# A transformer block's first segment: half of its modulation columns by tensor-engine products, and one written order for all engines

## The chip, the cores and the metric

The kernel runs on one core of a Trainium2 chip. The metric is the device time of one execution in microseconds. TensorE (PE in the profile, its weight loads PEld) multiplies, VectorE (DVE) and ScalarE (ACT) work elementwise, GpSimd (POOL) helps, and SyncE (SP) issues the transfers.

## The reference

The block takes 2048 tokens of width 1024. A vector `c` gives six modulation rows by a product with `w_mod`; two of them scale and shift the normalised input ahead of the attention, two ahead of the feed-forward part, and two gate the branches. The attention works in four segments of 512 tokens, each with softmax inside the segment and a memory of the segments before it.

```python
mod = (_silu(c) @ w_mod).reshape(c.shape[0], 6, 1, -1)
sa, ca, ga, sb, cb, gb = (mod[:, 0], mod[:, 1], mod[:, 2], mod[:, 3], mod[:, 4], mod[:, 5])
h = _layernorm(x, axis=-1) * (1 + ca) + sa
x = x + ga * _A_ref(h, A_wq, A_wk, A_wv, A_wo, A_beta)
h = _layernorm(x, axis=-1) * (1 + cb) + sb
x = x + gb * _B_ref(h, B_w_gate, B_w_up, B_w_down)
```

In `_A_ref`, q, k and v are products of h with 1024 x 1024 weights, 32 heads of 32; `_B_ref` is `(gelu(h @ w_gate) * (h @ w_up)) @ w_down` with 3584 hidden units.

## The kernel before

**Numbers.** Products with float32 accuracy are made of three float32r products: each operand is cut into a high half (a copy rounded to float32r, on ACT) and a low half (the difference, on DVE or POOL). `split_w` (L194 to L202) cuts weights, `mm` (L361) issues the three products of one block of 128 rows.

**The attention** goes through 32 steps (`steps`): for each half of the sequence and each of eight groups of four heads, two segments. A step has scores S, values V, memory M and A, and beside it the products K (v, then k) and Q of the next step; two written strings, `ORDER0` for the first step and `ORDER` for the others, interleave these pieces on TensorE. Weights of the next group are fetched and cut as entries of a list `todo` at positions of that string. After the steps come the output projection and the feed-forward part.

**Who sets the order.** TensorE runs in the order of the program throughout (`tc.manual_schedule`). In the first segment SP does so too. DVE, ACT and POOL there, and all but TensorE in the attention steps, are ordered by a planner that goes by its own costs and by what is ready; SP, and then the others, are in program order again in the feed-forward part. A wait between engines is a semaphore; a buffer of a pool (`tag`, `bufs`) is reused when its last reader is done.

**The first segment.** The set-up loads `ccol` (c), `bb` (beta), the eight half tiles of the first 512 tokens (`x0`), and the first group's weights wq, wv, wk into three of the four `raw` buffers. It makes selectors (`ident`, `pick`, `eye`, `sel4`, `selj`, `seli`, `blk`) and the causal `mask`, the silu of c (`scol`), a row copy of it in all partitions (`scb`, by `row_of`), and the gates (`gall`, `omg`).

A modulation column is 128 values of one row of `mod`; `modT[:, r]` holds column r, where columns 0 to 7 are the shift `sa` and 8 to 15 the scale `ca`, one of each for every block `kt` of 128 features. `mod_load` fetches 128 x 1024 values of the transposed `w_mod` (512 KB) into one of eight `spare` buffers; `mod_col` (L187) multiplies them by `scb` and sums along the row in one DVE instruction, and adds 1 to a scale. All sixteen columns of the first two rows are made so, in the order of `kt`:

```python
order = [r for kt in range(KT) for r in (8 + kt, kt)]
for i, r in enumerate(order):
    mod_col(*got[i])
    if i + 8 < len(order):
        got.append(mod_load(order[i + 8], spare[i % 8]))
```

`norm_seg_stats` normalises four tiles of tokens: statistics on DVE (L232 to L237), a power on POOL (L238), the scaling of both halves on ACT (L245). `norm_seg` (L325) turns a block of features by four transposes (L329), modulates it on ACT with columns `kt` and `8 + kt` (L331), and cuts it into high (L334, ACT) and low (L335, DVE). `first_part` multiplies each block with the three weights (L365, 72 products), and ends with `k_out`, `v_out`, `q_out` (copies and cuts of k, v and q), `k_turn` and `v_turn`. The transfers of k into `ks` are issued in `k_turn` (L395), those of q in `q_out` (L421). Meanwhile the second segment's tokens (`x1`, four `raw` buffers) are loaded and normalised; their `norm_seg` runs as the piece N of the first step. After `first_part` come the fills of the last 32 partitions of `ks` (L1361).

Of the kernel before, what the change touches and what calls it, by code (L numbers as in the profile page):

```python
# [11 lines left out]
F32 = mybir.dt.float32  # L12
# [7 lines left out]
P = 128  # L20
D = 1024
# [12 lines left out]


@with_exitstack
def block_kernel(ctx: ExitStack, tc: tile.TileContext, x, c, wmod, wq, wk, wv, wo, beta, wg, wu, wd, out):
    nc = tc.nc
    f32 = lambda ap: ap.bitcast(F32)

# [50 lines left out]

    ccol = cs([P, KT], "ccol")
    nc.sync.dma_start(ccol, c)
    bb = cs([P, H], "bb")
    nc.sync.dma_start(bb, bass.AP(tensor=beta.tensor, offset=beta.offset, ap=[[0, P], [1, H]]))
    def fetch(src, name):
        r = raw_tile("r" + name)
        nc.sync.dma_start(r, src)
        return r

    x0 = [[], []]
    for i in range(4):
        for h in range(2):
            tag, bufs = ("pt0", 4) if h == 0 else ("sj", 3) if i < 3 else ("pq", 2)
            t = t2(f"x0_{i}_{h}", tag, bufs=bufs)
            nc.sync.dma_start(t, x[i * P:(i + 1) * P, h * L:(h + 1) * L])
            x0[h].append(t)
    raw0 = [fetch(w[0], f"w0_{i}") for i, w in enumerate((wq, wv, wk))]


    ones = cs([P, P], "ones")
    nc.vector.memset(ones, 1.0)
    ident = cs([P, P], "ident")
    nc.gpsimd.affine_select(ident, ones, pattern=[[-1, P]], compare_op=ALU.is_equal, fill=0.0,
                            base=0, channel_multiplier=1)
    mask = pa.tile([P, L], F32, name="mask")
    nc.vector.memset(mask, 0.0)
    nc.gpsimd.affine_select(mask[:, L - P:], mask[:, L - P:], pattern=[[-1, P]],
                            compare_op=ALU.is_ge, fill=MASK, base=0, channel_multiplier=1)

    pick = tmp_tile("pick")[:, :P].rearrange("p (j d) -> p j d", d=DH)
    nc.gpsimd.affine_select(pick, ones.rearrange("p (j d) -> p j d", d=DH), pattern=[[-1, 4], [-4, DH]],
                            compare_op=ALU.is_equal, fill=0.0, base=0, channel_multiplier=1)
    sel4 = cs([P, 4], "sel4")
    nc.vector.tensor_reduce(sel4, pick, axis=AX.X, op=ALU.add)
    blk = pa.tile([P, P], F32, name="blk")
    nc.vector.tensor_copy(blk.rearrange("p (j e) -> p j e", e=DH), sel4.unsqueeze(2).to_broadcast([P, 4, DH]))

    eye = tmp_tile("eye")[:, :32].rearrange("p (j i l) -> p j i l", j=4, i=4)
    nc.gpsimd.affine_select(eye, ones[:, :32].rearrange("p (j i l) -> p j i l", j=4, i=4),  # L130
                            pattern=[[-8, 4], [-2, 4], [-1, 2]], compare_op=ALU.is_equal, fill=0.0,
                            base=-96, channel_multiplier=1)
    selj = cs([P, 4], "selj")
    nc.vector.tensor_reduce(selj, eye.rearrange("p j i l -> p j (i l)"), axis=AX.X, op=ALU.add)
    seli = cs([P, 4], "seli")
    nc.vector.tensor_copy(seli, eye[:, 0, :, 0])
    for j in range(4):
        for part in range(2):
            if j or part:
                nc.vector.tensor_add(seli, seli, eye[:, j, :, part])  # L140
    mhalf = cs([P, 4], "mhalf")
    nc.vector.memset(mhalf, -0.5)


    def sigmoid(dst, src):
        nc.scalar.activation(dst, src, AF.Exp, scale=-1.0)
# [18 lines left out]
    def row_of(*a):  # L165
        for _ in row_parts(*a):
            pass

    scol = cs([P, KT], "scol")
    sigmoid(scol, ccol)  # L170
    nc.vector.tensor_mul(scol, scol, ccol)
    scb = t2("scb", "row", shape=(P, D))
    row_of(scb, scol, tmp_tile, "sc")
    gall = cs([P, H], "gall")
    sigmoid(gall, bb)
    omg = pa.tile([P, H], F32, name="omg")
    nc.vector.tensor_scalar(omg, gall, -1.0, 1.0, op0=ALU.mult, op1=ALU.add)
    modT = cs([P, 48], "modT")

    def mod_load(r, w=None):  # L180
        if w is None:
# [133 lines left out]
            for _ in range(3):  # L315
                yield

    def norm_seg_stats(s, halves, tiles=range(4)):

        for i in tiles:  # L320
            mv, rs = norm_stats([halves[0][i], halves[1][i]], f"a{s}_{i}", s > 0)
            norm_scale([halves[h][i] for h in range(2)], mv, rs, f"{s}_{i}")
# [37 lines left out]
    def mm(i, ps, g, s, kt):  # L360
# [3 lines left out]
        for a, b in ((0, hi), (0, lo), (1, hi)):  # L364
            nc.tensor.matmul(ps, w[:, a], b, start=(kt == 0 and a == 0 and b is hi), stop=(kt == KT - 1 and a == 1))  # L365

    def v_out(n, nm, ps):
# [4 lines left out]
        ST[n] = [None, ks_t[n % 2], vx, None]  # L372
        return vr, vx

    def v_turn(nm, vr, vx):
# [5 lines left out]
    def k_out(s, nm, ps):  # L381
# [7 lines left out]
            nc.scalar.activation(kr, ps, AF.Copy)  # L389
        return kh, kl, kr  # L390

    def k_turn(n, s, nm, kh, kl, kr):
        ks = ks_t[n % 2]
        for qd, srct in ((0, kh), (1, kh), (2, kl)):
            nc.sync.dma_start(f32(ks[32 * qd:32 * qd + 32]), f32(srct))  # L395
        if s < NSEG - 1:
            ps = s_ps("kT" + nm)
            for t in range(4):
                nc.tensor.transpose(ps[:, t * P:(t + 1) * P], kr[:, t * P:(t + 1) * P], ident)
            e = tmp_tile("ek" + nm)  # L400
            nc.scalar.activation(e, ps, AF.Exp)
            nc.vector.tensor_scalar_min(e, e, 1.0)
            pk = t2("pk" + nm, "pk", shape=(P, 4, P))
            nc.vector.scalar_tensor_tensor(pk.rearrange("p a b -> p (a b)"), ps, 0.0, e, op0=ALU.max, op1=ALU.add)
            PK[n] = pk, ST[n][2]

    def q_out(n, s, nm, ps):
# [14 lines left out]
        ST[n][0], ST[n][3] = qs, pq  # L422

    def kv_part(n, g, s):

        nm = f"{g}_{s}"
        ps = mm_ps("v" + nm)
        for kt in range(KT):
            mm(1, ps, g, s, kt)
            if kt % 2 and kt < KT - 1:  # L430
                yield
        vr, vx = v_out(n, nm, ps)
        yield
        ps = mm_ps("k" + nm)
# [19 lines left out]
        q_out(n, s, nm, ps)  # L454
        yield

    def first_part(n, g, s):

        nm = f"{g}_{s}"
        pv, pk, pq = mm_ps("v" + nm), mm_ps("k" + nm), o_ps("q" + nm)  # L460
        for kt in range(KT):
            for i, ps in ((1, pv), (2, pk), (0, pq)):
                mm(i, ps, g, s, kt)
            yield
        kk = k_out(s, nm, pk)
# [868 lines left out]
    proj = projections()  # L1334
    gab = None
    with tc.manual_schedule(engines={mybir.EngineType.PE}):
        with tc.manual_schedule(engines={mybir.EngineType.SP}):
            free = [wsp_tile("wm_a"), wsp_tile("wm_b")] + [
                t2(f"wm_{q}", "qs", bufs=2, dt=F32R, shape=(P, 4, L)).rearrange("p (a b) t -> p a (b t)", a=2) for q in "cd"]
            spare = [f32(w[:, h]) for w in free for h in range(2)]  # L1340
            order = [r for kt in range(KT) for r in (8 + kt, kt)]
            got = [mod_load(r, spare[i]) for i, r in enumerate(order[:8])]
            norm_seg_stats(0, x0)
            W[0] = [None] * 3
            for i in (1, 2, 0):
                W[0][i] = split_w(raw0[i], wsp_tile(f"w0_{i}"), nc.vector)
            nseg = norm_seg(0, x0)
            for i, r in enumerate(order):
                mod_col(*got[i])
                if i + 8 < len(order):  # L1350
                    got.append(mod_load(order[i + 8], spare[i % 8]))
                if i in (1, 3):
                    next(nseg)
            x1h = [fetch(x[L + i * P:L + (i + 1) * P, :], f"x1_{i}") for i in range(4)]
            x1h = [[t[:, h * L:(h + 1) * L] for t in x1h] for h in range(2)]
# [4 lines left out]
        for k in ks_t:  # L1360
            nc.scalar.activation(k[96:128], selj[96:128].unsqueeze(2).to_broadcast([32, 4, L]), AF.Copy)  # L1361
        norm_a = norm_tiles(x, hT_d, (2, 3), 1, 0, "a")
        next(norm_a)
        for n in range(len(steps) + 1):
# [7 lines left out]
            work["N"] = norm_seg(1, x1h) if n == 0 else norm_a  # L1372
            side = none
            if n in (14, 15):
                hT[n - 12] = []
# [91 lines left out]
```

## Time and profile before

| what | value |
|---|---|
| median of 3 runs | 2791.91 us (2790.25 to 2795.36) |
| profiled execution | 2793.34 us |
| its span, first to last instruction | 2791.6 us |
| mean granted clock of TensorE | 0.994 |
| busy share | PE 98%, PEld 79%, DVE 63%, ACT 46%, POOL 19% |
| instructions | 38457 |
| moved by DMA | 480.17 MB, mean 172 GB/s |

The span is what the trace shows; the execution has 1.7 us around it. A busy share is an average over the whole span: the first segment is some 2% of it and looks different from the rest. In rows of the timeline the start and the length are in microseconds; "x3" counts the instructions in a row, and brackets hold the idle time ahead and what ended it.

### The profile page before, as it was taken

The page shows a single profiled execution, that of the slowest core. Times are in us where ns is not written, and L with a number is a line of the kernel's source. Part 1 is how long each engine was busy: PE and PEld are TensorE (multiplying, and loading weights), DVE is VectorE, ACT ScalarE, POOL GpSimd, SP SyncE. Part 2 cuts the span into 40 slices and gives each one's busy share as a digit, 9 for nine tenths or more (in the row PEclk, how much of TensorE's full clock was granted, in tenths as well). Part 3 has the DMA queues.
Part 4 walks back from the last instruction along what each step waited for, and adds up shares of the span by engine and source line. Part 5 has one row for each costly group of instructions (what it writes and reads, how often), then busy time and mean ns, then how long its engine had stood idle before and what let it go on. Part 6 is the DMA issues. An engine that isn't in the chain of part 4 may idle for free.

```text
span 2791.6 us, 38457 instructions
## 1 busy us (share of the span) xinstructions
PE 2726.0 (98%) x13276; PEld 2206.7 (79%) x13276; DVE 1762.9 (63%) x3727; ACT 1291.4 (46%) x2861; POOL 542.2 (19%) x986
## 2 busy tenths in 40 slices
PE   5999999999999999999999999999999999999999
PEld 4777777777777777788888887888888878888887
DVE  7566566766666744677776768666678754434543
ACT  6688776767676635233433324223223243232220
POOL 0333334333332531100000002000000002112432
PEclk8999999999999999999999999999999999999999
DMA  7566655666555547655655644343567685544652
GB/s 228 129 147 139 157 114 127 148 141 128 114 115 101 133 169 250 210 205 194 226 197 204 234 161 157 137 149 129 190 246 249 218 312 171 184 139 155 207 185 79
DMA packets 229606, 480.17 MB, mean 172 GB/s; under 512 B 17442, under 2 KB 92194, under 8 KB 229410
## 3 DMA queue, kind: packets, MB, share of 16 engines
q1 hardware_dynamic: 229408, 477.72, 56.9%
q8 instruction: 104, 1.70, 0.3%
q14 instruction: 94, 0.75, 0.1%
HBM read 300.96 MB, written 126.35 MB: 153 GB/s over the span
## 4 chain that ended last, share of the span: by engine, by line
PE 85%; DVE 7%; DMA 3%; ACT 2%; issue 2%; POOL 1%; SPq 0%; DVEq 0%; ACTq 0%; POOLq 0%
PE f L1126 36%; PE d L1292 19%; PE k L365 6%; PE q L365 5%; PE v L365 4%; PE y L630 3%; PE S L498 3%; PE O L571 3%; PE T L562 3%; DVE qs L515 1%; PE M L478 1%; PE R L585 1%; DVE sj L500 1%; DVE A L764 1%; PE num L536 1%
## 5 line engine op out<-in xcount | busy, mean ns | idle before, releaser
L1126 PE MATMUL f<-A,B 128*128 128x512 f32 x4704 | 1074.6, 390 | 4.9 <-DVE c L1091 3.2
L1126 PEld LDWEIGHTS f<-A,B 128*128 128x128 f32 x4704 | 882.6, 188 | 190.3 <-issue 2.9
L1292 PE MATMUL d<-wb,ah 128*128 128x512 f32 x2352 | 534.4, 389 | 1.0 <-DVE wb L1177 1.0
L1292 PEld LDWEIGHTS d<-wb,ah 128*128 128x128 f32 x2352 | 441.3, 188 | 93.8 <-DVE wb L1177 1.8
L500 DVE CUSTOM_DVE_ANT_0 sj<-S,mask 128x384 f32<-128x384 f32 (+3 forms) x512 | 227.9, 487 | 183.8 <-PE S L498 175.3
L502 ACT ACTIVATE sj<-sj,mm 128x384 f32<-128x384 f32 (+3 forms) x512 | 282.4, 556 | 27.5 <-DVE mm L500 25.2
L564 ACT ACTIVATE pt<-T 128x256 f32<-128x256 f32 (+3 forms) x512 | 184.9, 455 | 119.9 <-PE T L562 118.5
L1177 DVE TENSOR_TENSOR ah<-ar,ah 128x1792 fp32r<-128x1792 f32 x56 | 115.9, 2069 | 188.7 <-ACT ah L1176 188.7
L565 POOL TENSOR_SCALAR_AFFINE_SELECT pt<-pt 128x128 f32<-128x128 f32 x512 | 166.4, 344 | 341.4 <-ACT pt L564 334.3
L1176 ACT ACTIVATE ah<-ar 128x1792 fp32r<-128x1792 f32 x56 | 95.3, 1702 | 286.1 <-PE d L1292 244.2
L1093 ACT ACTIVATE g<-g 128x512 f32<-128x512 f32 x56 | 35.4, 632 | 303.1 <-DVE g L1093 303.1
L201 POOL TENSOR_TENSOR w<-r,w 128x256 fp32r<-128x256 f32 x180 | 133.1, 771 | 161.5 <-ACT w L196 161.4
L764 DVE TENSOR_TENSOR B<-t,B 128x512 fp32r<-128x512 f32 x168 | 116.0, 690 | 56.4 <-ACT B L767 56.3
L1200 POOL TENSOR_TENSOR yo<-u,gbb 128x256 f32<-128x256 f32 x32 | 29.8, 959 | 549.8 <-ACT gbb L162 547.7
L767 ACT ACTIVATE B<-t 128x512 fp32r<-128x512 f32 x168 | 105.5, 628 | 63.2 <-PE f L1126 59.7
L630 PE MATMUL y<-wo,hho 128*128 128x512 f32 x384 | 125.9, 393 | 1.0 <-DVE xr L634 1.0
L562 PE MATMUL T<-qs,ks 128*128 128x256 f32 (+2 forms) x512 | 114.6, 338 | 6.7 <-DVE qs L515 2.6
L562 PEld LDWEIGHTS T<-qs,ks 128*128 128x128 f32 x512 | 83.0, 188 | 47.0 <-issue 21.7
L1090 ACT ACTIVATE g<-f 128x512 f32<-128x512 f32 x56 | 33.5, 599 | 176.9 <-PE f L1126 176.9
L764 DVE TENSOR_TENSOR B<-rg,B 128x512 fp32r<-128x512 f32 x112 | 77.8, 695 | 53.0 <-ACT B L767 52.9
L498 PE MATMUL S<-ks,qs 96*128 96x256 f32 (+2 forms) x512 | 108.1, 332 | 1.2 <-DVE mm L500 1.2
L1218 POOL TENSOR_TENSOR xo<-xo,yo 128x256 f32<-128x256 f32 x64 | 70.1, 1123 | 195.6 <-DMA xo<-x_d 155.4
(232 smaller groups left out, 4338.9 us busy)
## 6 DMA issues: line engine op xcount, KB each, us to landing
ar<-hid_d SPq DMA_DIRECT2D x56, 896.0 KB, 5.1
rg<-wg SPq DMA_DIRECT2D x56, 512.0 KB, 4.8
ru<-wu SPq DMA_DIRECT2D x56, 512.0 KB, 5.6
hid_d<-g SPq DMA_DIRECT2D x56, 512.0 KB, 3.1
sc<-hid_d SPq DMA_DIRECT2D x56, 512.0 KB, 5.6
hid_d<-sc SPq DMA_DIRECT2D x56, 512.0 KB, 2.9
br<-wT_d SPq DMA_DIRECT2D x49, 512.0 KB, 6.0
qs<-qh SPq DMA_DIRECT2D x64, 256.0 KB, 4.8
```

Source lines behind the costliest of these rows:

```text
L201: eng.tensor_sub(w[:, 1, k:k + 256], r[:, k:k + 256], f32(w[:, 0, k:k + 256]))
L365: nc.tensor.matmul(ps, w[:, a], b, start=(kt == 0 and a == 0 and b is hi), stop=(kt == KT - 1 and a == 1))
L498: nc.tensor.matmul(ps[:, :nk], qs[:96, j, i * P:(i + 1) * P], ks[:96, j, :nk], start=True, stop=True)
L500: nc.vector.tensor_tensor_reduce(out=sj[:, :nv], in0=ps[:, :nv], in1=mask[:, L - nv:], scale=-1.0, scalar=3.4e38, op0=ALU.add, op1=ALU.min ...
L502: nc.scalar.activation(sj[:, :nv], sj[:, :nv], AF.Exp, bias=mm[:, j, i:i + 1], scale=-1.0, accum_out=ll[:, i, j:j + 1])
L562: nc.tensor.matmul(ps[:, :nn], ks[:, j, kc * P:(kc + 1) * P], qs[:, j, L - nn:], start=True, stop=True)
L564: nc.scalar.activation(pt, ps[:, nn - n:nn], AF.Exp)
L565: nc.gpsimd.affine_select(pt[:, :P], pt[:, :P], pattern=[[1, P]], compare_op=ALU.is_ge, fill=0.0, base=0, channel_multiplier=-1)
L630: nc.tensor.matmul(ps, b[:, i * P:(i + 1) * P], w[:, a, g % 2], start=(g == 0 and a == 0 and b is hi), stop=(g == G - 1 and a == 1))
L764: eng.tensor_sub(dst[:, k], a[:, k], b[:, k])
L1126: nc.tensor.matmul(ps, B[m, i][:, a, kt * P:(kt + 1) * P], A[p, i, kt][b], start=(start and kt == 0 and a == 0 and b == 0), stop=(kt == 3 ...
L1292: nc.tensor.matmul(ps[t], ops[n][:, x, k, t * P:(t + 1) * P], b[:, y, kk % 2], start=(kk == 0 and x == 0 and y == 0), stop=(kk == 13 and x ...
```

## The change

Everything from the selectors to the end of the first segment goes into one function, `start`, which runs with PE, SP, DVE, ACT and POOL in program order. `first_part` and `norm_seg_stats` go.

- The columns of blocks 0, 1, 4 and 5 (eight of sixteen) are made by products. A new input `wms` holds their weights, untransposed, in two sets of four transfers of 512 KB (`wms[0]` for blocks 0 and 1, `wms[1]` for 4 and 5). `scz` is `scol` with 31 columns of zeros behind each value, so that a product with it has 32 output rows; `mod_rows` adds the eight products of a set up in four column groups of the array, in two halves of four; ACT copies the result out, and `mod_cols` sums over the groups and turns the rows into columns by four products with `ones`. DVE then writes four columns of `modT`.
- The columns of blocks 2, 3, 6 and 7 are made by `mod_col` as before.
- Loads are in the order of use: c, x0, `wms[0]`, wv, rows 10 and 2, wk, wq, rows 11 and 3; then `wms[1]`, rows 14, 6, 15, 7, beta and x1 when buffers come free.
- The scaling in a normalisation is shared: one half of a tile on ACT, the other on DVE.
- `warm` multiplies `ones` by the mask into a buffer that is not read.
- `k_send` is taken out of `k_turn`; the fills of `ks` come first on ACT; the gates come last; the mask is made on POOL.
- Turns (`turn`), modulation and high half (`high`), low half (`low`) and products (`products`) of the blocks are interleaved by hand.

```diff
-            got = [mod_load(r, spare[i]) for i, r in enumerate(order[:8])]
-            norm_seg_stats(0, x0)
-            for i in (1, 2, 0):
-                W[0][i] = split_w(raw0[i], wsp_tile(f"w0_{i}"), nc.vector)
...
-            for kt, _ in enumerate(first_part(0, 0, 0)):
-                next(nseg, None)
-                if kt >= 4:
-                    norm_seg_stats(1, x1h, (kt - 4,))
+        with tc.manual_schedule(engines={mybir.EngineType.SP, mybir.EngineType.DVE, mybir.EngineType.Activation,
+                                         mybir.EngineType.Pool}):
+            norm_1 = start()
...
+    def start():
...
+        for d in range(4):
+            nc.sync.dma_start(spare[d], wms[0, d])
+        raw = {1: fetch(wv[0], "w0_1")}
+        got = {kt: [mod_load(r, spare[2 * kt + q]) for q, r in enumerate((8 + kt, kt))] for kt in (2,)}
+        for i in (2, 0):
+            raw[i] = fetch((wq, wv, wk)[i][0], f"w0_{i}")
+        got[3] = [mod_load(r, spare[6 + q]) for q, r in enumerate((11, 3))]
...
+        def normal(halves, name, engs):
+            st = []
+            for i in range(4):
+                if i > 1:
+                    scale(i - 2, halves, *st[i - 2], name, engs)
+                st.append(norm_stats([halves[0][i], halves[1][i]], f"{name}{i}"))
+                yield
+            for i in (2, 3):
+                scale(i, halves, *st[i], name, engs)
...
+        def mod_rows(m, part):
+            if part == 0:
+                mod_ps[m] = s_ps(f"md{m}")
+            ps = mod_ps[m]
+            for kt in range(4 * part, 4 * part + 4):
+                j = 32 * (kt % 4)
+                nc.tensor.matmul(ps[j:j + 32], scz[:, kt], spare[kt // 2][:, kt % 2 * L:(kt % 2 + 1) * L],
+                                 start=(kt < 4), stop=(kt >= 4), skip_group_check=True)
+            if part == 1:
+                mod_ps[m] = tmp_tile(f"mr{m}")
+                nc.scalar.activation(mod_ps[m], ps, AF.Copy)
+
+        def mod_cols(m):
+            ps = s_ps(f"mt{m}")
+            for q in range(4):
+                nc.tensor.matmul(ps[:, q:q + 1], mod_ps[m][:, q * P:(q + 1) * P], ones[:, :1], start=True, stop=True)
+            nc.vector.tensor_scalar_add(modT[:, 8 + 4 * m:10 + 4 * m], ps[:, 0:4:2], 1.0)
+            nc.vector.tensor_copy(modT[:, 4 * m:4 * m + 2], ps[:, 1:4:2])
...
+        def products(*kts):
+            for i in (1, 2, 0) if kts[-1] < KT - 1 else (2, 0, 1):
+                for kt in kts:
+                    mm(i, ps[i], 0, 0, kt)
+
+        warm(1)
+        cut(1)
+        mod_rows(0, 0)
+        warm(1)
+        mod_rows(0, 1)
+        warm(1)
+        turn(0)
+        turn(1)
+        mod_cols(0)
+        for d in range(4):
+            nc.sync.dma_start(spare[d], wms[1, d])
+        high(0)
+        mod_col(*got[2][0])
+        low(0)
+        high(1)
+        mod_col(*got[2][1])
+        low(1)
+        cut(2)
+        cut(0)
+        turn(2)
+        turn(3)
+        warm(3)
+        high(2)
+        mods(3)
+        low(2)
...
+        products(0, 1)
+        mod_rows(1, 0)
+        products(2)
+        high(3)
+        low(3)
+        mod_rows(1, 1)
+        turn(4)
+        turn(5)
+        mod_col(*got[6][0])
+        mod_cols(1)
+        high(4)
+        mod_col(*got[6][1])
+        products(3)
+        high(5)
+        low(4)
+        turn(6)
+        mod_col(*got[7][0])
+        low(5)
+        high(6)
+        mod_col(*got[7][1])
+        low(6)
+        products(4)
+        turn(7)
+        high(7)
+        next(norm)
+        products(5)
+        low(7)
+        products(6, 7)
+        next(norm)
+        kk = k_out(0, nm, ps[2])
+        k_send(0, *kk)
+        q_out(0, 0, nm, ps[0])
+        next(norm)
+        vv = v_out(0, nm, ps[1])
+        for _ in norm:
+            pass
+        k_turn(0, 0, nm, *kk)
+        v_turn(nm, *vv)
...
+        return norm_seg(1, x1h)
```

More of the change, by code (lines that the diff above doesn't have):

```diff
@@ L36, in block_kernel @@
 @with_exitstack
-def block_kernel(ctx: ExitStack, tc: tile.TileContext, x, c, wmod, wq, wk, wv, wo, beta, wg, wu, wd, out):
+def block_kernel(ctx: ExitStack, tc: tile.TileContext, x, c, wmod, wms, wq, wk, wv, wo, beta, wg, wu, wd, out):
     nc = tc.nc
@@ L99, in fetch @@
         return r
[L101 to L108, printed above, removed]
     ones = cs([P, P], "ones")
-    nc.vector.memset(ones, 1.0)
     ident = cs([P, P], "ident")
-    nc.gpsimd.affine_select(ident, ones, pattern=[[-1, P]], compare_op=ALU.is_equal, fill=0.0,
-                            base=0, channel_multiplier=1)
@@ L116, in block_kernel @@
     mask = pa.tile([P, L], F32, name="mask")
[L117 to L123, printed above, removed]
@@ L133, in block_kernel @@
     selj = cs([P, 4], "selj")
-    nc.vector.tensor_reduce(selj, eye.rearrange("p j i l -> p j (i l)"), axis=AX.X, op=ALU.add)
     seli = cs([P, 4], "seli")
[L136 to L140, printed above, removed]
-    mhalf = cs([P, 4], "mhalf")
-    nc.vector.memset(mhalf, -0.5)
+    mhalf = cs([P, 4], "mhalf")
+    bb = cs([P, H], "bb")
+    gall = cs([P, H], "gall")
@@ L145, in sigmoid @@
+    omg = pa.tile([P, H], F32, name="omg")
+    modT = cs([P, 48], "modT")
+    scol = cs([P, KT], "scol")
+    scb = t2("scb", "row", shape=(P, D))
     def sigmoid(dst, src):
@@ L167, in row_of @@
             pass
[L169 to L178, printed above, removed]
     def mod_load(r, w=None):
@@ L316, in norm_tiles @@
                 yield
[L318 to L322, printed above, removed]
     def norm_seg(s, halves):
@@ L365, in mm, with state @@
             nc.tensor.matmul(ps, w[:, a], b, start=(kt == 0 and a == 0 and b is hi), stop=(kt == KT - 1 and a == 1))
+    def state(n):
+        return ST.setdefault(n, [None, ks_t[n % 2], None, None])
     def v_out(n, nm, ps):
@@ L371, in v_out @@
         nc.gpsimd.memset(vx[:, :, P:], 1.0)
-        ST[n] = [None, ks_t[n % 2], vx, None]
+        state(n)[2] = vx
         return vr, vx
@@ L390, in k_out, with k_send @@
         return kh, kl, kr
+    def k_send(n, kh, kl, kr):
+        for qd, srct in ((0, kh), (1, kh), (2, kl)):
+            nc.sync.dma_start(f32(ks_t[n % 2][32 * qd:32 * qd + 32]), f32(srct))
     def k_turn(n, s, nm, kh, kl, kr):
-        ks = ks_t[n % 2]
-        for qd, srct in ((0, kh), (1, kh), (2, kl)):
-            nc.sync.dma_start(f32(ks[32 * qd:32 * qd + 32]), f32(srct))
         if s < NSEG - 1:
@@ L442, in kv_part @@
         yield
+        k_send(n, *kk)
         k_turn(n, s, nm, *kk)
@@ L1371, in block_kernel @@
                 work["M"] = memory(n, *steps[n][1:])
-            work["N"] = norm_seg(1, x1h) if n == 0 else norm_a
+            work["N"] = norm_1 if n == 0 else norm_a
             side = none
@@ L1445 @@
     wo = np.asarray(A_wo).reshape(4, 2, P, 2, 512).transpose(3, 0, 2, 1, 4)
+    wm = np.asarray(w_mod).reshape(KT, P, 6, KT, P)
+    wms = np.stack([wm[:, :, (1, 0, 1, 0), (0, 0, 1, 1)], wm[:, :, (1, 0, 1, 0), (4, 4, 5, 5)]])
     arrays = {
@@ L1449 @@
         "wmod": np.asarray(w_mod).T.reshape(48, P, D),
+        "wms": wms.reshape(2, 4, 2, P, L).transpose(0, 1, 3, 2, 4).reshape(2, 4, P, D),
         "wq": cols(np.ascontiguousarray(by_head(A_wq)).reshape(D, D), P),
```

130 lines of the change are left out of this document (92 added, 38 removed).

## The prediction, made before the changed kernel was run

> **What bounds the kernel now.** I read the page first, then busy time by stage, then the chain of waits of the first 75 us, then the groups and the timeline for prices. In the window rows the columns are the stretch, its length, busy us and instruction count of PE, PEld, DVE, ACT and POOL, the granted clock, the DMA share and GB/s.
>
> ```profile
> span 2791.6 us, 38457 instructions
> PE 2726.0 (98%) x13276; PEld 2206.7 (79%) x13276; DVE 1762.9 (63%) x3727; ACT 1291.4 (46%) x2861; POOL 542.2 (19%) x986
> 0.00:10.00 10.00, 0.00 (x0) 0.00 (x0) 5.20 (x19) 1.72 (x3) 2.08 (x12) 1.00 0.70 231
> 10.00:20.00 10.00, 5.90 (x12) 2.52 (x12) 7.19 (x30) 9.68 (x13) 1.65 (x3) 0.85 1.03 412
> 20.00:30.00 10.00, 4.44 (x10) 3.06 (x11) 10.00 (x16) 6.38 (x7) 0.00 (x0) 0.50 1.01 381
> 30.00:40.00 10.00, 6.61 (x27) 5.25 (x26) 10.00 (x23) 2.82 (x4) 0.00 (x0) 0.84 0.96 352
> 40.00:53.80 13.80, 13.12 (x63) 10.18 (x61) 8.37 (x18) 8.25 (x12) 0.95 (x2) 0.97 0.08 32
> 53.80:73.20 19.40, 13.06 (x64) 10.42 (x65) 11.87 (x24) 15.61 (x25) 1.33 (x3) 0.82 0.86 157
> 73.20:110.00 36.80, 32.61 (x162) 25.54 (x161) 18.07 (x60) 23.50 (x61) 15.74 (x30) 0.95 0.54 118
> 110.00:1010.00 900.00, 884.81 (x5120) 692.32 (x5119) 591.20 (x1972) 648.83 (x1839) 335.93 (x747) 1.00 0.60 131
> ```
>
> TensorE is idle for 65.6 us of the span, and the first 110 us hold 34.3 of them (10.0, 4.1, 5.6, 3.4, 0.7, 6.3 and 4.2 by stage). From 20 to 40 us VectorE is full. The chain of waits (start, length, what) shows what the array waits for.
>
> ```profile
> 15.41 2.87 ACT x L245 x5
> 21.05 2.35 DVE w L198 x2
> 23.41 1.13 DVE wm_b L187
> 36.37 0.61 DVE hla L335
> 37.88 1.28 PE k L365 x3
> 44.38 0.70 PE k L365 x3
> 51.60 1.21 DVE sta L232 x2
> 60.43 0.82 ACT rx L245
> 61.30 5.08 PE tpa L329 x29
> 66.52 6.46 DMA r<-wv
> 53.38 0.39 PE L365 MATMUL q<-hha,w 128*128 128x512 f32 x1
> 72.97 0.39 PE L365 MATMUL v<-hha,w 128*128 128x512 f32 x1
> ```
>
> Up to 37 us the set-up hangs on VectorE: weight cuts (L198), then modulation columns (L187) and the low halves hla (L335). The segment's 72 products then run one after another and end at 53.8 (53.38+0.39). The second segment's four normalisations, each with its statistics (L232), end at 61.25 (60.43+0.82); its turns (tpa) follow, and its first products end at 73.4. The same three products take 1.28 us at 37.88 and 0.70 at 44.38: 0.43 us each on the slow clock, 0.232 on the full one.
>
> **The change, part by part.** These are the prices (name, shapes, count | busy us, mean ns | idle before), with four rows of the timeline.
>
> ```profile
> L331 ACT ACTIVATE h<-tpa,modT 128x512 f32<-128x512 f32 x16 | 12.4, 777 | 15.2 <-PE tpa L329 13.7 <-DVE modT L192 1.4
> L187 DVE CUSTOM_DVE_ANT_0 wm_d<-wm_d,scb 128x1024 f32<-128x1024 f32 x4 | 4.8, 1213 | 0.0
> L196 ACT ACTIVATE w<-rw 128x1024 fp32r<-128x1024 f32 x3 | 2.9, 1047 | 0.0
> L384 ACT ACTIVATE kh<-k 128x512 fp32r<-128x512 f32 x1 | 0.6, 598 | 0.1
> L402 DVE TENSOR_SCALAR ek<-ek 128x512 f32<-128x512 f32 x1 | 0.4, 427 | 0.0
> L192 DVE TENSOR_SCALAR modT<-modT 128x1 f32<-128x1 f32 x8 | 1.2, 147 | 0.1
> L243 DVE TENSOR_SCALAR mr<-mva,rsa 128x1 f32<-128x1 f32 x8 | 1.7, 214 | 2.7 <-POOL rsa L238 2.6
> L238 POOL TENSOR_TENSOR rsa<-rsa,mhalf 128x1 f32<-128x1 f32 x8 | 4.5, 560 | 53.1 <-ACT hha L334 35.2 <-DVE rsa L237 18.0
> L401 ACT ACTIVATE ek<-kT 128x512 f32<-128x512 f32 x1 | 0.6, 573 | 0.0
> 40.23 0.93 PE L329 MATMUL tpa<-ident,x 128*128 128x128 f32 x4
> 43.09 0.60 PE L329 MATMUL tpa<-ident,x 128*128 128x128 f32 x4
> 105.44 1.71 PE L571 MATMUL O<-pt,vx 128*32 128x512 f32 x16
> 79.44 1.06 PE L478 MATMUL M<-vx,pk 128*128 128x130 f32 x8
> ```
>
> *Removed from VectorE:* eight of sixteen columns. Back to back one costs 1.13 us, or about 1.2 where one is added (L192): 9.3 us. *Added on TensorE:* two sets of eight products of 128*32 by 512, four column groups at a time. The nearest row has 16 passes of 512 and 384 columns in 1.71 us; at 512 throughout, 1.95 us a set, about 1.0 per half and 1.8 per half on the slow clock. A set's four column turns are eight passes: 1.06 us, double when slow. Each set also adds a 0.6 us ScalarE copy and two small VectorE operations (0.3).
>
> *Transfers.* Eight loads of 512 KB are replaced by eight of the same size, so the bytes stay; SP's order changes. By 10 us 2.31 MB have come, then 0.41 MB/us. In the new order the inputs (2.10 MB) and the first block wms[0] (4.19 MB in all) are there at 14.6, wv at 15.9, rows 10 and 2 at 18.4, wk and wq at 20.9, rows 11 and 3 at 23.5, wms[1] at 28.6, rows 14 and 6 at 31.2, rows 15 and 7 at 33.8, the second segment's four tiles at 38.9. SP waits for the first set's products before wms[1], and rows 14 to 7, beta, x1 and then the sends of k and q queue behind that wait; six loads (rows 10, 2, wk, wq, rows 11, 3) are still to land then, so the queue does not run dry. The reloads of rows 14/6 and 15/7 wait for two used columns each, at 23.9 and 29.2 below, with earlier loads still in flight.
>
> *Up to the first columns.* Normalising the first segment is shared between ACT and DVE: half a tile costs 0.43 us on DVE beside 0.82 on ACT, so the tiles are ready before the set's products, which wait for 14.6. The second half set ends at 16.4, its copy on ACT stands behind wv's cut (15.9 plus 1.05) and ends at 17.6. Two turned blocks (0.6 each) and the column turns (1.06) end at 19.5, two VectorE operations at 19.9; with all of it slow 2 us later. The array has pauses here, so I take 20.9, the middle, and keep 19.9 and 21.9.
>
> *VectorE from 20.9,* in its written order: column 10 to 22.1, low half 0 to 22.7, column 2 to 23.9, low half 1 to 24.5, two cuts (2.35) to 26.8, columns 11 and 3 to 29.2, low halves 2 and 3 to 30.4, column 14 (data at 31.2) to 32.4. ACT's part of each block (0.78 and 0.63) lies beside it.
>
> *TensorE.* The q products of blocks 0 and 1 wait for the last cut and end at 28.2. First half of set two: 29.2. Block 2, waiting for low half 2 at 29.8: 31.7. Second half: 32.7. Two turned blocks: 33.9. Column turns: 35.0. VectorE waits here, from 32.4 on: column 6 stands behind these columns in its order, and low half 4, column 15 and all later low halves queue behind it. It goes on at 35.3: column 6 to 36.4, low half 4 to 37.0, column 15 to 38.2, low half 5 to 38.8, column 7 to 40.0, low half 6 to 40.6, one tile's statistics (1.4) to 42.0, low half 7 to 42.6. TensorE meanwhile: block 3 (nine products, 2.09) to 37.1, turn 37.7, block 4 to 39.8, turn 40.4, block 5 to 42.5, blocks 6 and 7 (18 products, 4.2) to 46.7. So TensorE's own work, not the columns, sets the end: 7.1 us ahead of 53.8.
>
> *The second segment.* k is complete at 43.9, q at 45.3. VectorE: a tile's statistics to 44.0, kl (kh at 44.5) to 45.1, ql to 46.5, then scalings of 0.6 (mr 0.2, half a tile 0.43) and statistics of 1.4 in turn: 47.1, 48.5, 49.1, 50.5, 51.1; the last waits for the power on POOL (0.56) and ends at 51.8, ACT's half at 52.2. That is 9.05 us ahead of 61.25. ek (0.57), which lay ahead of this in the old order, now stands behind it on ACT, ahead of the eight evictions that pace the turns: 8.5 us are left. k is sent ahead of its turn, which costs nothing: scores start only at 73.2. The same cover hides the moved gates (sigmoid of beta, omg), the selector fills of ks (ACT had nothing to do before 9 us) and the mask on POOL; without cover these are below 2 us together.
>
> *Sum.* After the turns all four raw buffers come free as before, the weights wv, wk, wq of the next group are fetched (66.52) and cut, and each of these steps hangs on the step before it, so the gain is carried. The profiled execution took 2793.34 us (span 2791.6 and 1.7 around it): 2793.34 - 8.5 = 2784.8. The median of the runs, 2791.91, is 1.43 lower: 2783.4.
>
> **The rivals.** The clock of the array is the disputed price; the last row is two products in plain float32, a pass 0.44 us, without groups.
>
> ```profile
> 61.30:62.00 0.70, 0.70 (x4) 0.70 (x5) 0.00 (x0) 0.70 (x2) 0.00 (x0) 0.50 0.98 126
> 64.00:65.00 1.00, 1.00 (x7) 1.00 (x6) 0.69 (x1) 1.00 (x3) 0.00 (x0) 0.60 1.09 131
> 65.00:66.00 1.00, 1.00 (x12) 1.00 (x11) 0.69 (x1) 1.00 (x3) 0.00 (x0) 1.00 1.08 131
> 37.03 0.50 PE L365 MATMUL v<-hla,w 128*128 128x512 f32 x1 [3.39 <-DVE hla L335]
> 2269.92 1.88 PE L161 MATMUL gb<-gbdg,ones 128*128 128x512 f32 x4
> ```
>
> *Rival 1, a cold spell: about the same.* If the turns ahead of blocks 0 and 1 do not raise the clock, the columns come at 21.9 (1.0 later than taken) and 12 of the 18 products wait little but cost 0.2 us more each (2.4): 3.4 us of the gain go, 5.1 stay, 2786.8. One more pause of 3.4 us as at 37.03, after which nine products and four turns were slow (9 times 0.2 and 0.3), costs 2.1: 2788.9. Against it: from 61.30 to 66 only turns ran, and the clock rose from 0.50 to 1.00 during them. The Trainium skill, "TensorE: Matmul & The Clock Gate", Part 4, says that transposes in transpose mode do not bring the array to its full clock; these rows do not agree with that for this kernel's turns, so by the rows turns count and 2783.4 holds, and by the rule it would be this rival's time. 0.14.
>
> *Rival 2, column groups run one after another: the same.* Unshared, a half set of eight passes costs 3.5 us instead of 1.0: 2.5 us more ahead of the first columns (the first half starts at 12 already) and 5.0 in the second set, together 7.5 of the 8.5: 2790.9. The L571 row speaks against it: 16 passes, unshared about 6 us (0.44 scaled to a mean of 448 columns), took 1.71. This is also how the change would fail to do what it says. 0.05.
>
> *Rival 3, the order behind the start: gain given back.* Behind the first segment only TensorE's order is written out; DMA issues, DVE, ACT and POOL are put in order by a planner with its own clock, which now starts from another point. From 110 to 1010 us TensorE is idle for 15.2 us; a new order that adds half of that again leaves under 1 us: 2791. It can as well take some away. 0.09.
>
> *Rival 4, slower: the array stays slow through the whole first segment.* Between 22 and 46 us it now gets its work in small pieces with waits for VectorE between them. If it never comes to full clock, 72 products cost 0.2 us more each (14.4), turns, sets and column turns another 4: 18.4 together, the segment ends near 65, 11 us later than 53.8, and the whole takes 2801.8. It decides when more than three quarters of the products are slow. Against it: between 40 and 53.8 us the array worked in pieces of nine with a clock of 0.97. 0.06.
>
> **How the numbers follow.** 0.66 for the forecast, 0.14, 0.05, 0.09 and 0.06 for the rivals. No change means within 0.2% (5.6 us, about what a measurement of this kernel can tell): above 2786.3 is no longer faster. The first rival lies across that edge, half on each side; of the third a sixth is faster, half the same, a third slower. Faster: 0.66, less 0.03 for a forecast that comes out short, plus 0.07 and 0.01: 0.71. Slower 0.06 + 0.03 = 0.09. Same: 0.20. The forecast's own range is 2781 to 2786: with the columns at 19.9 and ek beside other work the gain is 11, with them at 21.9 and the second set slow it is 6. The range for 8 in 10 is 2780 to 2791: the first three rivals inside for the most part, the slow one outside.
>
> **What would show it.** In the profile after: the first columns by product near 21 us; the last product of the first segment near 47; the first turn of the second segment near 52 to 53; its last first product near 65; VectorE waiting once, about 32 to 35, for the column turns of set two; the sets at 1 us a half; clock 1.00 from 25 on. It is wrong if the granted clock between 25 and 45 is well under 1, if the sets take several us, or if the idle time from 110 to 1010 (moved by the gain) is far from 15 us.

## The result and the profile after

The changed kernel took 2776.95 us (median of 6, 2775.34 to 2779.04) where the kernel before took 2793.49 beside it (6 runs): ratio 0.9943, 95% interval 0.9931 to 0.9956, or 15.9 us less (12.3 to 19.3). The prediction was 2783.4, range 2780 to 2791: the sign and the place were right, the size was not. The profiled execution took 2777.42 us.

The page, and busy time by stage of the changed kernel, with the stages cut at the same events as before (first products of the second segment, first scores, first turn of R, end of the steps):

```profile
span 2775.6 us, 38577 instructions
PE 2729.4 (98%) x13336; PEld 2206.0 (79%) x13336; DVE 1760.7 (63%) x3719; ACT 1287.3 (46%) x2855; POOL 542.0 (20%) x988
```

```profile
10.00:20.00 10.00, 7.70 (x43) 3.65 (x43) 7.60 (x21) 5.89 (x9) 1.98 (x3) 1.00 1.03 417
20.00:30.00 10.00, 9.01 (x42) 5.41 (x40) 8.82 (x15) 7.12 (x10) 0.00 (x0) 1.00 1.03 408
30.00:40.00 10.00, 10.00 (x60) 7.65 (x59) 7.47 (x16) 4.87 (x9) 0.00 (x0) 1.00 0.90 356
40.00:46.10 6.10, 5.77 (x26) 4.39 (x25) 4.81 (x12) 2.90 (x5) 1.40 (x2) 1.00 0.16 40
46.10:64.80 18.70, 13.43 (x65) 10.61 (x64) 13.92 (x31) 13.90 (x23) 1.27 (x5) 0.82 0.89 170
64.80:102.00 37.20, 35.25 (x196) 27.74 (x195) 19.60 (x72) 25.37 (x69) 13.44 (x29) 1.00 0.50 102
102.00:998.00 896.00, 879.70 (x5083) 687.90 (x5082) 590.25 (x1963) 646.59 (x1829) 335.43 (x746) 1.00 0.60 132
998.00:2775.60 1777.60, 1764.31 (x7831) 1456.87 (x7829) 1101.08 (x1569) 575.37 (x901) 185.89 (x193) 1.00 0.55 192
```

The same view of the kernel before, from its first scores on:

```profile
73.20:114.20 41.00, 36.81 (x195) 28.80 (x193) 20.03 (x70) 26.05 (x70) 16.53 (x33) 0.96 0.52 113
114.20:1009.00 894.80, 879.61 (x5083) 688.15 (x5080) 589.24 (x1963) 645.83 (x1829) 334.13 (x741) 1.00 0.60 132
1009.00:2791.60 1782.60, 1766.49 (x7832) 1458.30 (x7831) 1101.01 (x1569) 575.02 (x901) 185.53 (x194) 1.00 0.55 191
```

Read the lengths. The start is 8.4 us shorter (64.8 against 73.2), as forecast. Then come two stretches that the prediction took as unchanged: from the first scores to the first turn of R 37.2 instead of 41.0, with the clock at 1.00 instead of 0.96; and behind the steps 1777.6 instead of 1782.6. The long middle is 1.2 longer. The experiments give the first of the two a cause; how much of the second is scatter between executions stays open.

The start, in the timeline of the changed kernel:

```profile
14.66 1.99 PE L515 MATMUL md<-wm_b,scz 128*32 128x512 f32 x8
...
19.62 0.15 DVE L526 COPY modT<-mt 128x2 f32<-128x2 f32 x1
...
27.45 1.07 PE L515 MATMUL md<-wm_a,scz 128*32 128x512 f32 x8
31.23 1.07 PE L515 MATMUL md<-wm_b,scz 128*32 128x512 f32 x8
34.14 0.16 DVE L525 TENSOR_SCALAR modT<-mt 128x2 f32<-128x2 f32 x1 [1.31 <-PE mt L524]
45.67 0.39 PE L318 MATMUL v<-hha,w 128*128 128x512 f32 x1
53.60 1.49 ACT L284 ACTIVATE h<-tpa,modT 128x512 f32<-128x512 f32 x2
64.56 0.39 PE L318 MATMUL v<-hha,w 128*128 128x512 f32 x1
64.79 0.64 PE L658 MATMUL S<-ks,qs 96*128 96x256 f32 x4
```

The chain of waits names what carried it (start, length, what):

```profile
52.29 0.81 ACT rx L486
53.10 0.48 ACT ek L358
53.58 0.12 ACT gall L116
53.70 0.57 ACT h L284
```

The last normalisation ends at 53.1; ek and the gate stand behind it on ScalarE, ahead of the first eviction of the turns. In the kernel before, ScalarE had the second half of the last tile to scale at that place, which is VectorE's now:

```profile
60.43 1.52 ACT L245 ACTIVATE rx<-rx,mr,rsa 128x512 f32<-128x512 f32 x2 [1.15 <-DVE mr L243]
61.86 1.65 ACT L331 ACTIVATE h<-tpa,modT 128x512 f32<-128x512 f32 x2
```

### The profile page after: what moved, and what is told of

It reads as the page before. It is cut to its first block, busy times and chain, and to the rows that moved or that the text cites. A ratio compares the mean times of both kernels' runs of the same rounds, so it can differ in the third digit from the quotient of the medians.

```text
span 2775.6 us, 38577 instructions
## 1 busy us (share of the span) xinstructions
PE 2729.4 (98%) x13336; PEld 2206.0 (79%) x13336; DVE 1760.7 (63%) x3719; ACT 1287.3 (46%) x2855; POOL 542.0 (20%) x988
## 4 chain that ended last, share of the span: by engine, by line
PE 86%; DVE 6%; issue 2%; ACT 2%; DMA 1%; POOL 1%; SPq 0%; DVEq 0%; ACTq 0%; POOLq 0%
PE f L1286 36%; PE d L1452 19%; PE k L318 6%; PE q L318 5%; PE y L790 5%; PE v L318 3%; PE S L658 3%; PE O L731 3%; PE T L722 3%; DVE qs L675 1%; PE M L638 1%; DVE sj L660 1%; PE R L745 1%; PE num L696 1%; PE vT L334 0%
## 5 line engine op out<-in xcount | busy, mean ns | idle before, releaser
L927 ACT ACTIVATE B<-t 128x512 fp32r<-128x512 f32 x168 | 105.4, 628 | 63.7 <-PE f L1286 60.0
```

## The experiments

Landmarks of every profiled execution, in us of its own timeline: first scores S, start of the first and of the last turn of R, and the lengths between them; "kT waits" is TensorE's wait before the turns of k of the second step. Labels with b_ are the kernel before with an edit (b_again and b_again2: none), those with a_ the changed one (after_again: none).

| run | S | kT waits | S to first R | S to last R | last R to end |
|---|---|---|---|---|---|
| before | 73.2 | 3.56 | 41.0 | 935.7 | 1782.7 |
| b_again | 74.6 | 3.36 | 41.8 | 936.0 | 1780.0 |
| b_again2 | 73.3 | 3.68 | 41.1 | 936.8 | 1778.8 |
| b_wms | 74.3 | 6.00 | 44.7 | 938.9 | 1778.7 |
| b_fix | 73.3 | 1.96 | 38.3 | 938.2 | 1781.9 |
| b_fix2 | 73.3 | 1.95 | 37.3 | 932.5 | 1781.3 |
| after | 64.8 | 1.27 | 37.2 | 932.9 | 1777.9 |
| after_again | 64.5 | 1.26 | 37.2 | 933.1 | 1780.1 |
| a_allcols | 72.9 | 1.27 | 37.1 | 932.6 | 1778.6 |
| a_allcols_nowms | 72.3 | 1.27 | 37.1 | 931.0 | 1777.7 |
| a_onegroup | 71.8 | 1.27 | 37.2 | 933.1 | 1778.0 |
| a_nowarm | 65.4 | 1.27 | 37.1 | 932.3 | 1777.1 |
| a_actscale | 64.8 | 1.27 | 37.1 | 931.1 | 1776.8 |
| a_normfirst | 63.7 | 1.27 | 37.1 | 932.1 | 1778.7 |

**a_allcols: all sixteen columns on VectorE, in the new order.** The sets and column turns are gone; the same bytes are loaded as rows of `wmod`.

```diff
-            nc.sync.dma_start(spare[d], wms[0, d])
+            nc.sync.dma_start(spare[d], wmod[(8, 0, 9, 1)[d]])
...
         def mod_cols(m):
+            for d in range(4):
+                mod_col(((8, 0, 9, 1), (12, 4, 13, 5))[m][d], spare[d])
+            return
```

> The changed kernel with all sixteen columns made by VectorE again (the eight blocks of wms replaced by eight rows of wmod of the same size at the same places of the queue, no products for columns), everything else in its written order. Theory 1 (VectorE's eight columns were what mattered): VectorE gets 9.3 us more and loses 0.6, TensorE loses some 5 us of work ahead of the last product; the last product of the first segment, 46.1 in after, comes at 52 to 53, the first scores at 71 instead of 64.8, the whole at 2783 to 2784. Rival (the written order and the order of loads were what mattered): within 2 us of after, 2777 to 2779.

Measured: 2784.89 us, ratio 0.9972 (0.9960 to 0.9983). Its first scores and the turns behind them, in the timeline:

```profile
72.93 0.64 PE L662 MATMUL S<-ks,qs 96*128 96x256 f32 x4
...
88.15 0.66 PE L356 MATMUL kT<-ident,kn 128*128 128x128 f32 x4 [1.27 <-ACT kn L345]
```

Two things follow. In the first segment, and in this order, the columns are worth 8.1 us and the written order with its loads 0.3 by these two traces (about 1 by the means of the table, 73.7 for the six with the old start and 72.6 for the two a_allcols): VectorE's 9.3 us were the term that counted. Yet this kernel, whose first scores come as late as before, is 7.8 us faster than before (4.7 to 11.2): a second gain came with the new function and does not come from the columns.

**a_onegroup: the products of a set one after another, in one column group.**

```diff
-                j = 32 * (kt % 4)
+                j = 0
...
-                                 start=(kt < 4), stop=(kt >= 4), skip_group_check=True)
+                                 start=(kt < 1), stop=(kt >= 7), skip_group_check=True)
```

The copy and the column turns then read the 32 rows of that group alone.

> The changed kernel with the eight products of a set added up in one column group of 32 instead of four groups side by side. It prices the sharing: by the prediction's second rival a half set costs 3.5 us instead of 1.0, so 2.4 more ahead of the first columns and 5.0 in the second set, 7.4 together: first scores at 72.2, the whole at 2784.4. If VectorE still sets the pace in the second set, only the first 2.4 and a part of the 5.0 show: 2780 to 2782. If the groups never ran side by side: no change, 2777.

Measured: 2784.95 us, ratio 0.9970 (0.9960 to 0.9981); first scores at 71.8, 7.0 later than with four groups.

```profile
11.46 3.62 PE L515 MATMUL md<-wm_a,scz 128*32 128x512 f32 x8 [1.03 <-DMA wm_a<-wms]
```

Eight passes take 3.62 us here and 1.07 in four groups (the row at 27.45). That is the price and the consequence (7.5) that the second rival named; it did not happen, because the groups do run beside each other. The Trainium skill, "TensorEngine Tiling (Array Packing)", Overview, gives up to four times for a dimension of 32; 3.62 over 1.07 is 3.4 here.

**a_nowarm: without the products that only keep the array busy.**

```diff
         def warm(n):
+            return
```

> The changed kernel without the products that only keep the array busy (warm). By the prediction's reading of the old trace, turns count as work for the clock, but here 2 us of turns and column products alone stand ahead of block 0. If the clock is at full rate all the same at 21 us: within 1 us of after, 2777. If not, by the first rival of the prediction, 12 of the first 18 products cost 0.2 us more each and the sets and turns ahead are slow too: 3 to 4 us more at the first scores (68 instead of 64.8), 2780 to 2781. By the rule of the Trainium skill (TensorE: Matmul & The Clock Gate, Part 4) the second is to be expected.

Measured: 2776.40 us, ratio 0.9945 (0.9932 to 0.9957); first scores 0.6 later, at 65.4. By stage:

```profile
14.00:18.00 4.00, 4.00 (x18) 1.23 (x16) 2.18 (x8) 2.83 (x4) 0.66 (x1) 0.69 1.03 418
18.00:20.00 2.00, 1.68 (x16) 1.61 (x16) 1.63 (x4) 0.54 (x2) 0.00 (x0) 1.00 1.01 404
...
24.00:26.00 2.00, 2.00 (x5) 1.59 (x6) 2.00 (x3) 1.77 (x3) 0.00 (x0) 0.50 1.04 416
26.00:28.00 2.00, 2.00 (x8) 1.59 (x7) 1.97 (x4) 0.00 (x0) 0.00 (x0) 0.81 1.01 401
```

So the first rival's cold spell is real without these products, around 16 and again around 25, but little of it reaches the end: 0.6 us instead of 3.4. The first spell costs nothing, since the first column turns, which wait for ScalarE's copy, start at 18.39 here and at 18.46 with the products; behind the second the column turns of set two start 0.6 later (33.78 against 33.16). By 18 us sets and turns alone had brought the clock from 0.69 to 1.00. The Trainium skill, "TensorE: Matmul & The Clock Gate", Part 4, says that transposes in transpose mode do not bring the array to its full clock; these windows mix turns with the sets and cannot decide that. The rows from 61.30 to 66 in the prediction, with turns alone, show the clock rise to 1.00; whether this kernel's turns run in that mode no trace shows.

**a_actscale: both halves of a normalisation scaled on ScalarE.** `normal(x0, "a0", (nc.scalar, nc.scalar))`, and the same for `x1h`.

> The changed kernel with both halves of each tile scaled on ScalarE, as in before, for both segments. VectorE loses eight operations of 0.43 to 0.55 us. First segment: VectorE waits for transfers around 16 us, so nothing is gained there, and ScalarE ends the four tiles up to 1.5 us later, still ahead of wv's cut at 16.9: no change to within 0.5. Second segment: VectorE's chain ends 2 us sooner but the last tile's second half waits on ScalarE 0.8 us longer, which is what the turns wait for: 0 to 1 us at the first scores. The whole 2776 to 2778.

Measured: 2775.56 us, ratio 0.9942 (0.9929 to 0.9954), first scores at 64.8 as in the changed kernel: the shared scaling moves nothing.

**Where the second gain comes from.** ScalarE, SP and TensorE of the kernel before, in the timeline:

```profile
78.36 1.99 ACT L196 ACTIVATE w<-r 128x1024 fp32r<-128x1024 f32 x2
...
85.18 0.33 SPq L98 DMA_DIRECT2D r<-wv  x1
85.48 0.58 ACT L384 ACTIVATE kh<-k 128x512 fp32r<-128x512 f32 x1
89.55 1.06 ACT L196 ACTIVATE w<-r 128x1024 fp32r<-128x1024 f32 x1 [3.49 <-DMA r<-wv]
90.51 0.58 ACT L389 ACTIVATE kn<-k 128x512 f32<-128x512 f32 x1
91.14 0.66 PE L399 MATMUL kT<-ident,kn 128*128 128x128 f32 x4 [3.56 <-ACT kn L389]
```

And of the changed kernel:

```profile
76.66 0.57 ACT L340 ACTIVATE kh<-k 128x512 fp32r<-128x512 f32 x1
77.13 1.04 ACT L155 ACTIVATE w<-r 128x1024 fp32r<-128x1024 f32 x1
79.36 0.60 ACT L345 ACTIVATE kn<-k 128x512 f32<-128x512 f32 x1 [1.18 <-DVE kl L341]
80.01 0.66 PE L356 MATMUL kT<-ident,kn 128*128 128x128 f32 x4 [1.27 <-ACT kn L345]
...
84.99 0.54 SPq L97 DMA_DIRECT2D r<-wv  x1
```

Before, ScalarE has made the last cuts of the next group's weights by 80.4 (78.36 and 1.99). Between kh and kn the planner then put the cut of the group after that, whose load is issued only at 85.18. ScalarE stands for 3.49 us at that cut; kn, which needs nothing of it, is queued behind, and TensorE waits for kn. In the changed kernel the place between kh and kn is taken by a weight cut whose data are there, and the next load is issued well after kn. The written order ends with the first segment; what stands here is what the planner made of a start that came out otherwise. All eight traces with the new start have this order, a_allcols among them; which part of the new start led the planner to it was not tested.

**b_again: the kernel before, unchanged.**

> The kernel before, unchanged, for a second look at one execution. From 1009 us (end of the attention steps) to the end, the profiled execution of before took 1782.6 us and that of after 1778.0: 4.6 us of the 16.0 between the two spans lie where both run the same work in the same order on TensorE. Theory 1 (that part is scatter between executions, and the change is worth 11.4 to 12.3): the second look gives another length of this stretch, anywhere from 1778 to 1784. Theory 2 (the changed order of the queues is worth 4.6 there as well): it repeats within 1 us, 1782 to 1783.5. Both expect the first scores at 73.2, the turn of step 1's k at 91.1 behind a wait of 3.6 us, and the last values of the steps at 1008 to 1009.

Measured: 2792.33 us, with the same order: a wait of 3.36 and 41.8 from S to the first R. The wait is not an accident of one execution, though its length scatters: ScalarE stood 3.27 us for the load here, and 5.92 in b_wms further below, where the order is the same and TensorE's wait was 6.00.

**b_fix: the kernel before, with that cut on ScalarE held to its place in the program.**

```diff
-        nc.scalar.activation(w[:, 0], r, AF.Copy)
+        keep(nc.scalar.activation(w[:, 0], r, AF.Copy))
```

(`keep` is the scheduler's "in program order" for the cut of wv of group 2 alone.)

> The kernel before with one instruction held back on ScalarE: the high half of the weight cut for group 2's v stays in program order instead of being taken forward between kh and kn of step 1. Theory 1 (between 73 and 105 us the gain grew from 8.4 to 12.3 because in before kn stood on ScalarE behind that cut, whose load was issued only at 85.2, and the array lost its full clock in the wait): the wait of 3.6 us at the turn of k falls to about 1.3, the clock stays at 1.00 between 90 and 100, and the whole is 3 to 4 us shorter, 2790 against 2793.5. Rival (the load and its cut are late for all that use them, and the wait only moves to the next product): no change within 1 us.

Measured: 2793.07 us, ratio 1.0 (0.999 to 1.0009). The wait fell to 1.96 and S to R to 38.3, but the steps ended no earlier: S to last R is 938.2. The edit shifted ScalarE's order further on; at 206.83 another cut stands before its load, and TensorE waits right behind it. From the timeline and from the waits of TensorE, 200 to 215 us (total, times, longest):

```profile
206.83 1.06 ACT L196 ACTIVATE w<-r 128x1024 fp32r<-128x1024 f32 x1 [3.72 <-DMA r<-wq]
```

```profile
PE S L498 <- DVE mm L500: 2.4, 1, 2.4
```

From the first to the last R this kernel took 899.9 us, 5.3 more than before (894.6). The wait shown is 2.4 of them; 2.5 more are lost between 111.5 and 171.6, and what causes these was not followed. The local mechanism was shown, the gain was not: the edit took one wait away and made at least one other of the same kind. This is the third rival's picture, in a kernel where nothing else was changed.

**b_fix2: the same cut, queued right behind kn.**

```diff
-            W[g][i] = split_w(raws[i], wsp_tile(f"w{i}_{half}_{g}"))
+            with (tc.issue_after(ST["kn0_1"]) if (half, g, i) == (0, 2, 1) else ExitStack()): ...
```

> The kernel before, with one edit: on ScalarE the cut of group 2's v weight is queued behind the kn of step 1, by an edge on the issue order, and not held to its place in the program; it lands two places later in ScalarE's queue (kh, kn, rx, cut where it was kh, cut, kn, rx). Theory 'the late cut ahead of kn costs the steps 3 to 4 us': the wait before the turns of step 1 falls from 3.56 us to below 2, the clock of 88 to 100 stays at 1.00, first scores to first R turn falls from 41.0 to about 38, and, since no cut stands late this time, the end of the steps (1008.9) moves up by 3 to 4 us and the median to about 2789. Rival 'what is won here is given back by a later wait of the order that the planner writes', as in the other edit of this kind: the first R turn is earlier by 3, the end of the steps is not, and the median stays at 2792 to 2793.

Measured: 2788.32 us, ratio 0.9980 (0.9971 to 0.9988), or 5.6 us less (3.4 to 8.1). Its timeline, its clock from 88 to 100, and that of the kernel before in the same window:

```profile
85.63 0.58 ACT L384 ACTIVATE kh<-k 128x512 fp32r<-128x512 f32 x1
89.01 0.60 ACT L389 ACTIVATE kn<-k 128x512 f32<-128x512 f32 x1 [2.81 <-DVE kl L385]
89.66 0.66 PE L399 MATMUL kT<-ident,kn 128*128 128x128 f32 x4 [1.95 <-ACT kn L389]
90.03 1.05 ACT L196 ACTIVATE w<-r 128x1024 fp32r<-128x1024 f32 x1
```

```profile
88.00:100.00 12.00, 10.34 (x48) 8.72 (x49) 5.80 (x14) 7.32 (x12) 4.56 (x9) 1.00 0.97 146
```

```profile
88.00:100.00 12.00, 8.86 (x34) 7.24 (x35) 5.78 (x14) 4.72 (x8) 3.73 (x6) 0.86 0.83 117
```

With the columns, the loads and the start as before, one cut moved two places behind gives 932.5 from S to the last R, as in the changed kernels (931.0 to 933.1), against 935.7 to 936.8 in the three executions of the kernel before (mean 936.1). Of these 3.6 us 1.6 are the wait (3.56 to 1.95) and 1.7 the clock: 12 us at 0.86 instead of 1.00. This is the second gain, taken alone.

**b_wms and a_allcols_nowms: the new input alone.** The change adds an input of 4.19 MB, so what is allocated behind it may lie elsewhere; that might have moved the stretch behind the steps. b_wms adds the input, unused, to the kernel before; a_allcols_nowms takes it out of a_allcols.

> The kernel before with one more input of the size of wms (4 MB), at its place among the inputs, that nothing reads. All queues stay as in before. It asks where the 3.4 us come from that all versions of the changed kernel gain behind the attention steps (1009 us to the end: 1782.8, 1780.0 and 1781.9 us in three looks at the old start, 1777.9, 1778.6 and 1778.0 at the new one). Theory 1 (the addresses of all that follows wms in memory move, and transfers of the feed-forward part come sooner): the stretch takes 1777.5 to 1779 us and the whole 2789 to 2789.5. Theory 2 (the order of the queues, or the phase in which the stretch is reached): 1780 to 1783 us, the whole unchanged, 2792.6.

> The kernel with the new order and all columns on VectorE, now without the input wms, which it did not read. The other half of the same question. Theory 1 (addresses): the stretch from 1009 us on takes 1780 to 1783 us instead of 1778.6, the whole 2788 instead of 2784.9. Theory 2 (order): no change within 1 us.

Measured: 2791.89 (ratio 0.9999, 0.9990 to 1.0008) and 2783.29 (0.9969, 0.9958 to 0.9980), which is what the kernels without the edit took. The input does nothing to the time that these runs could tell. The last stretch was 1778.7 in b_wms and 1777.7 in a_allcols_nowms.

**after_again and b_again2: is the stretch behind the steps shorter after the change?**

> The changed kernel, once more, for a second look at the stretch behind the steps. Theory 'the changed start leaves that stretch shorter in every execution': end of the steps to the end of the span at 1776.8 to 1778.6 as in the six looks so far with the new start, and the cut of step 1's kn again with a wait of 1.27 us and a clock of 1.00 in 90 to 100. Rival 'that stretch scatters from execution to execution, and the new start has only met its short side': 1779 to 1783 as in three of four looks with the old start.

> The kernel before, once more, for a third look. Theory as for the changed kernel's second look: behind the steps 1779 to 1783, and a wait of 3.4 us or more before the turns of step 1 with a clock below 0.90 behind it. Rival of scatter: 1777 to 1779 here, as in one of four looks so far.

Measured: 2779.52 us with 1780.1, and 2790.57 with 1778.8: the other way round. "Shorter in every execution" falls. With the old start the stretch took 1778.7 to 1782.7 in six executions (mean 1780.6), with the new one 1776.8 to 1780.1 in eight (mean 1778.1). Part of it is scatter; whether the 2.5 us between the means are more than that stays open. One source of scatter can be seen: the same wait in two executions of the kernel before, b_again and then b_again2, each by its timeline row and its window.

```profile
1725.85 2.74 PE L1126 MATMUL f<-A,B 128*128 128x512 f32 x6 [1.92 <-DVE c L1091]
```

```profile
1720.00:1740.00 20.00, 17.40 (x68) 13.22 (x67) 17.11 (x26) 7.55 (x15) 4.50 (x4) 0.91 0.44 158
```

```profile
1725.57 2.80 PE L1126 MATMUL f<-A,B 128*128 128x512 f32 x11 [1.92 <-DVE c L1091]
```

```profile
1720.00:1740.00 20.00, 17.34 (x73) 13.05 (x72) 18.28 (x28) 7.26 (x14) 4.34 (x4) 1.00 0.43 158
```

After 1.92 us of waiting the clock fell in the one (0.91 over 20 us) and not in the other; products that start behind it take 0.46 or 0.25 us (2.74 by 6, 2.80 by 11).

**a_normfirst: the second segment's first scaling ahead of the cut of q.**

```diff
-        q_out(0, 0, nm, ps[0])
-        next(norm)
+        next(norm)
+        q_out(0, 0, nm, ps[0])
```

> The changed kernel, with the first scaling of the second segment's tiles put ahead of the cut of q (DVE: mra and rx_0 before ql; ACT: rx_0 before qh). In the changed kernel VectorE idles about 1 us at 44.8 to 45.9, waiting for qh. Theory 'the normalisation of segment 2 sets the first scores': up to 1 us earlier at the last normalisation (53.1) and at the first scores (64.8), so 2776 where the changed kernel had 2776.95. Rival 'the chain of q (qh, ql, its transfers) is as late': first scores at 64.8 or up to 1 us later, 2777 to 2778. Less than one us of 2777 is at the edge of what five rounds tell; the first scores in the trace decide.

Measured: 2775.94 us, ratio 0.9937 (0.9923 to 0.9950); first scores at 63.7, 1.1 earlier. Normalisation of the second segment sets that time, as the prediction's chain had it. This version is nominally 1 us better than the changed kernel; the intervals overlap, so only the timeline shows it.

## Why the prediction was right about the start and wrong about the time

*The start: right, by its steps.* First columns at 19.8 (taken: 20.9, bounds 19.9 to 21.9, so the early end and a little better). Half a set takes 1.07 us once its weights are there (set two); in set one the second half takes 1.99, with a wait for a load inside. VectorE waits for the column turns of set two once, 32.8 to 34.1 (32.4 to 35.3 forecast), with two shorter waits ahead of it (0.97 for a high half, 0.62 for a load). Last product of the first segment 46.06 (46.7). Last normalisation 53.1 (52.2: q's low half waits 1.2 us for its high half, which VectorE's list took as ready). First products end at 64.95 ("near 65"). Clock 1.00 from 10 to 46. The gain at the first scores was 8.4, forecast 8.5, but the agreement to 0.1 is partly luck, as two terms of that sum were off and offset each other. The last normalisation gained 8.15 (61.25 to 53.10) where 9.05 was forecast. And ek, priced at 0.57 of that gain, cost nothing in sum: 61.25 is the end of the first half tile only, and before, ScalarE went on with the second half until 61.95. That half is VectorE's now, ek and the gate take its place, and the first eviction starts 8.26 earlier (61.86 to 53.60).

*The rivals.* The cold spell did not come, and would have cost 0.6 instead of 3.4 had the warming products been missing. Column groups one after another cost 7.0 where 7.5 was said. The array was not slow through the segment.

*The step that failed* is the last of the sum: "each of these steps hangs on the step before it, so the gain is carried." It was carried, but the stretch behind it did not stay as it was. The prediction's own row from 73.20 to 110 showed 4.2 us of idle and a clock of 0.95, and nothing in the prediction asks what TensorE waits for there: kn, behind a cut ahead of its load. That order is the planner's, and the planner was given another start. Rival 3 named just this, but priced it only as a loss, and in the wrong place: the idle time of 110 to 1010, which it would have had grow from 15.2, is 16.3 in the changed kernel, hardly moved. "It can as well take some away" had neither a price nor a chance; b_fix2 measures it at 3.6 us in the trace and 5.6 (3.4 to 8.1) in the runs. The prediction also counted from the median of three runs, 2791.91, where six gave 2793.49; so it missed the time by 6.4 us, but the gain by 7.4 (15.9 where 8.5 was forecast).

*What is left.* Three traces of the kernel before and two of the changed one, in the mean: S 73.7 and 64.6 (9.1), S to last R 936.1 and 933.0 (3.1), the rest 1780.5 and 1779.0 (1.5). That is 13.7 of the 15.9, inside the interval of 12.3 to 19.3. So 9 us are the start, the forecast mechanism, and some 3 to 4 the cut; 1.5 to 2.5 behind the steps are not explained, and neither are the 2.2 by which these few traces fall short of the runs.

## What to carry to other kernels

Where a planner orders the queues behind an edit, read that stretch for work queued ahead of what it blocks: a row such as "ACT waits 3.49 for a DMA", followed by an instruction that needs none of it, is a stall that any change upstream may remove or bring back, and it belongs in the forecast with both signs. Do one such reordering by itself (b_fix2: one cut, two places) before crediting the gain to the work that was removed. And keep an edit of the order as local as it can be: b_fix and b_fix2 took the same wait away, and only b_fix2, whose steps behind it stayed as long as before (895.2 from the first to the last R, against 894.6), kept the gain.

## What the runs showed of the hardware that was not expected

- A wait also costs behind itself: around and behind one of 3.56 us the clock averaged 0.86 from 88 to 100 (1.7 us lost), with one of 1.95 us there it stayed at 1.00 (b_fix2). The loss does not go by the length alone: with a wait of 3.36 us at the same place b_again had 0.72 in that window.
- That is no fixed threshold: in two executions of one kernel the same wait of 1.92 us was followed by a clock of 0.91 over 20 us in one and by 1.00 in the other. The Trainium skill, "TensorE: Matmul & The Clock Gate", Part 1, has a free-running window of activity of some 3.4 us, so that the point of change varies from run to run; that agrees with the scatter, while its condition of an idle window of that length was not met by a wait of 1.92 us alone.
